# In a fused attention and MoE kernel, the second chunk's scores move behind the previous pair's values

## Chip, cores and metric

The kernel runs on one core of a Trainium2 chip. The metric is the device time of one execution in microseconds (us). PE is TensorE, ACT ScalarE, DVE VectorE, POOL GpSimd, SP SyncE.

## The reference

Three stages in float32: attention of 4 batches x 12 heads (448 tokens, 64 wide) with a tanh cap on the scores; a mixture of 8 experts, one for each of the 1792 tokens; and a soft mixture with 32 slots.

```python
def _attn_ref(q, k, v, cap):
    scale = 1.0 / np.sqrt(q.shape[-1])
    scores = scale * np.matmul(q, k.transpose(0, 1, 3, 2))
    scores = cap * np.tanh(scores / cap)
    scores = scores - np.max(scores, axis=-1, keepdims=True)
    attn = np.exp(scores)
    attn = attn / (np.sum(attn, axis=-1, keepdims=True) + 1e-09)
    return np.matmul(attn, v).astype(np.float32)
...
    attn_out = _attn_ref(**attn_kwargs)
    x = np.ascontiguousarray(attn_out.transpose(0, 2, 1, 3)).reshape(B * S, H * D)
    x = _moe_ref(x=x, **moe_kwargs)
    return _moe2_ref(x=x, **moe2_kwargs)
```

The MoE stage takes each token's expert by the largest logit of x @ w_gate plus a bias, and multiplies gate * relu(x @ w1) @ w2.

## The kernel before, in words

The order of the instructions on each engine is the order in which the program is written; every engine works its queue in that order and waits on semaphores.

Attention goes over 24 pairs of heads (`for p in range(NPAIR)` in `attention`, 6 pairs a batch). Scores are held transposed: 448 keys by 448 queries, the keys in chunks of 128. Chunks 0, 1 and 2 are full; what is left of both heads, 64 keys each, is one short chunk. `scores(p, c, dst)` makes one chunk: q and k are each split into a high and a low part (`split`, on DVE), and a score is the sum of three products (kh and qh, kh and ql, kl and qh), for a full chunk one matmul per head, so six. They go into a tile of `ps_s`, a PSUM pool with two buffers; then ACT applies tanh (line 571) from there into SBUF. After two chunks one exp goes over both (`pexp`, line 574): over chunks 0 and 1 into `pt`, over the short chunk and chunk 2 into `pm`.

One turn p of the loop gives PE, in this order:

1. `scores1(p)`: chunk 0, chunk 1, and on ACT the exp of both;
2. `pv(p - 1)` (line 606): the values of the pair before, six matmuls, the chunks 0, 1, 2 for two heads, into `o_ps`. Chunks 0 and 1 read `pt`, chunk 2 reads `pm`. `ps_o` has one buffer;
3. `post2(p - 2)`: row sums and gate logits (`r_ps`, line 488), a transpose of the values (`x_ps`, line 495);
4. `pv2(p - 1)` (line 610): the values of the short chunk;
5. `scores2(p)`: the short chunk; a transpose (`rt_ps`, line 501); `scores3(p)`: chunk 2 and the exp of `pm`.

DVE has in a turn: `adds2(p - 1)` (adds chunk 2's exp), `split(p + 1)`, the copy of `r_ps`, `adds1(p)` (adds the exps of chunks 0 and 1, so it waits for `pexp`), `post1(p - 1)` (line 614: empties `o_ps`), and `post3` (line 503 on), which scales x; SP stores x and then loads q, k and v of a pair two turns ahead. In PSUM `ps_s` takes four banks, `ps_m` two, `ps_o` and `ps_x` one each.

When a batch's six pairs are done, `route_batch` gives four steps of routing (logits, best expert, ranks, a selection matrix `bsel`) that are put into the following turns; three batches fall into the loop, the fourth behind it.

Behind attention stand the experts (`item`), which split their weights in the same way and multiply three times, and then the soft mixture, which streams weights of 768 KB a unit through a ring of buffers.

Of the kernel before, what the change touches and what calls it, by code (L numbers as in the profile page):

```python
# [9 lines left out]
F32 = mybir.dt.float32  # L10
# [42 lines left out]
def attn_moe_softmoe(ctx, tc, qT, kT, vP, cap, modality, w_gate, mod_bias, w1, w2, w2t, phi, m2_w1, m2_w2, out):  # L53
# [3 lines left out]
    B, NP_, _, HD, S = qT.shape  # L57
# [46 lines left out]
    def tt(out, in0, in1, op, eng=None):  # L104
        (eng or nc.vector).tensor_tensor(out=out, in0=in0, in1=in1, op=op)  # L105
# [110 lines left out]
    def m2_load(i, pieces=1):  # L216
        src, slot = m2_src(i), m2_slot(i)
        m2_tiles[i] = slot.rearrange("p (k f) -> p k f", f=512 if i < 4 * E else H2)
        if pieces == 1:
            nc.sync.dma_start(slot, src)  # L220
            return []
        h = UNIT // pieces
        return [call(nc.sync.dma_start, slot[:, h * k:h * k + h], src[:, h * k:h * k + h]) for k in range(pieces)]

    def call(f, *a):
        return lambda *b: f(*a, *b)
# [211 lines left out]
    a1 = Slices(arena)  # L438
# [8 lines left out]
    def gather(col, rows=None):  # L447

        lim = {} if rows is None else {"bounds_check": rows - 1, "oob_is_err": False}
        for i in range(NT):  # L450
            nc.gpsimd.indirect_dma_start(out=xg[:, i, :], out_offset=None, in_=x_dram if rows is None else x_dram[:rows],  # L451
                                         in_offset=bass.IndirectOffsetOnAxis(ap=idx[:, col + i:col + i + 1], axis=0),
                                         **lim)
# [89 lines left out]
    def weights_first():  # L543
        e_first.append(load_e(NI + 3))
        for s in range(NRW):
            wload("A", s, e_first[-1])

    def attention(a1, a1q, a2p, first, ps_s, ps_o, ps_x, ps_m, item_start):
        raw, spl, pt_t, pt_m, o_t, part = dict(first), {}, {}, {}, {}, {}

        def split(p):
            spl[p] = split_qk(a1q, *raw[p][:2])

        def product(ps, k, p, row_sets):
            qh, ql, kh, kl = spl[p]
            for t, (kk, qq) in enumerate(((kh, qh), (kh, ql), (kl, qh))):
                for o, r in row_sets(ps):
                    nc.tensor.matmul(o, lhsT=kk[r, k], rhs=qq[r], start=(t == 0), stop=(t == 2))  # L558

        def by_heads(ps):  # L560

            return [(ps[:, h, :S], slice(HD * h, HD * h + HD)) for h in range(2)]

        def together(ps):

            return [(ps[:, 0, :S], slice(0, 128))]

        def scores(p, c, dst):
            ps = ps_s.tile([128, 2, 512], F32, tag="s", name="s_ps")
            product(ps, slice(KC * c, KC * c + KC), p, by_heads if c < NKC else together)  # L570
            nc.scalar.activation(out=dst, in_=ps[:, :, :S] if c < NKC else ps[:, 0, :S], func=AF.Tanh)  # L571

        def pexp(t):
            nc.scalar.activation(out=t, in_=t, func=AF.Exp, scale=capb)  # L574

        def scores1(p):
            pt = pt_t[p] = a1.tile([128, 2, 2, S], F32, tag="pt", name="pt", bufs=3)
            for c in range(2):
                scores(p, c, pt[:, c])
            pexp(pt)  # L580

        def scores2(p):
            pt_m[p] = a1.tile([128, 3, S], F32, tag="pm", name="pm", bufs=3)
            scores(p, NKC, pt_m[p][:, 0])

        def scores3(p):
            scores(p, 2, pt_m[p][:, 1:3])
            pexp(pt_m[p])

        def adds1(p):  # L590

            part[p] = a1.tile([128, 2, S], F32, tag="t1", name="t1", bufs=3)
            tt(part[p], pt_t[p][:, 0], pt_t[p][:, 1], ALU.add)

        def adds2(p):
            t, m = part.pop(p), pt_m[p]
            tt(t, t, m[:, 1:3], ALU.add)
            sums[p] = [(onesel[:, 0], t[:, 0]), (onesel[:, 1], t[:, 1]), (onesel[:, 2], m[:, 0])]

        def pv(p):  # L600
            vt = raw[p][2]
            o = o_t[p] = ps_o.tile([128, S], F32, tag="o", name="o_ps")
            for c in range(NKC):
                for h in range(2):
                    hd = slice(HD * h, HD * h + HD)
                    nc.tensor.matmul(o[hd], lhsT=vt[:, c, hd], rhs=pt_t[p][:, c, h] if c < 2 else pt_m[p][:, 1 + h],  # L606
                                     start=(c == 0), stop=False)

        def pv2(p):
            nc.tensor.matmul(o_t[p], lhsT=raw[p][2][:, NKC], rhs=pt_m[p][:, 0], start=False, stop=True)  # L610

        def post1(p):
            xt = a1.tile([128, S], F32, tag="xt", name="xt", bufs=2)
            nc.vector.tensor_copy(xt, o_t.pop(p))
            xun[p] = xt

        extra = {0: late_consts, 1: call(set_guard, 1e-9 * math.exp(-CAP_SMALL)), 2: later_consts, 4: last_consts}
        extra.update({5 + i: call(nc.vector.memset, xg[:, i], 0.0) for i in range(NT)})
        extra[9] = zero_c
        n2 = 0  # L620
        spl[0] = first_split
        later = []
        for p in range(NPAIR):
            if p + 2 < NPAIR:
                raw[p + 2] = load_qkv(a1, a1q, p + 2)
            if p >= 4 and p % 2 == 0 and n2 < NRING + 1:
                m2_load(n2)
                n2 += 1
            scores1(p)
            if p >= 1:  # L630
                pv(p - 1)
                adds2(p - 1)
            if p + 1 < NPAIR:
                split(p + 1)
            if p >= 2:
                post2(p - 2, a1, ps_x, ps_m)
            if later:
                later.pop(0)()
            if p >= 1:
                pv2(p - 1)  # L640
            scores2(p)
            adds1(p)
            if p >= 1:
                post1(p - 1)
            if p >= 2:
                post3(p - 2, a1, ps_m)
            scores3(p)
            if p in extra:
                extra[p]()
            if later:  # L650
                later.pop(0)()
            if p >= 2 and (p - 2) % NP_ == NP_ - 1:
                b = (p - 2) // NP_
                rb = route_batch(b, a2p, ps_m)
                later += rb
                if b == NB1 - 1:
                    f = route_first(a2p, ps_m)
                    later[-2] = lambda: (rb[-2](), f[0]())
                    later += [f[1], lambda: [g() for g in f[3:-1] + f[2:3]], lambda: (f[-1](), gather(NA, NB1 * S), weights_first()),
                              lambda: None, lambda: None]  # L660
                later.pop(0)()
        while later:
            later.pop(0)()
        assert n2 == NRING + 1 and a1.end <= UNIT * (NRINGA - 1)
        wsplits, xpreps = item_start()
        wsplits[0]()
        xscale(NA, True)
        pv(LAST)
        adds2(LAST)
        post2(LAST - 1, a1, ps_x, ps_m)  # L670
        wsplits[1]()
        for f in xpreps[:3]:
            f()
        pv2(LAST)
        for f in xpreps[3:5]:
            f()
        post1(LAST)
        xpreps[5]()

    def load_qkv(a1, a1q, p, eng=None):  # L680
        b, hp = divmod(p, NP_)
        qr = a1q.tile([128, S], F32, tag="qr", name="qr", bufs=2)
        kr = a1q.tile([128, S + KL], F32, tag="kr", name="kr", bufs=2)
        vt = a1.tile([128, NKC + 1, 2 * HD], F32, tag="vt", name="vt", bufs=4)
        (eng or nc.sync).dma_start(kr, kT[b, hp])
        nc.sync.dma_start(qr, qT[b, hp].rearrange("h d s -> (h d) s"))
        nc.sync.dma_start(vt, vP[b, hp])
        return qr, kr, vt

    def split_qk(a1q, qr, kr, act=False):  # L690

        qh, ql, kh, kl = (a1q.tile([128, w], F32R, tag=n, name=n, bufs=2)
                          for n, w in (("qh", S), ("ql", S), ("kh", S + KL), ("kl", S + KL)))
        if act:
            nc.scalar.copy(kh, kr)
        else:
            nc.vector.tensor_copy(kh, kr)
        ts(qh, qr, qsc, ALU.mult)
        stt(ql, qr, qsc, qh.bitcast(F32), ALU.mult, ALU.subtract)
        tt(kl, kr, kh.bitcast(F32), ALU.subtract)  # L700
        return qh, ql, kh, kl
# [797 lines left out]
```

## Time and profile before

| | |
|---|---|
| runs shown, us | 528.33, 532.64, 536.36 (median 532.64) |
| the profiled execution, us | 529.52 |
| its span, first to last instruction, us | 527.8 |
| mean granted TensorE clock | 0.976 |
| busy in the span: PE, DVE, ACT, POOL | 90%, 52%, 47%, 14% |
| HBM traffic | 112.52 MB read, 11.71 MB written |

The span is what the trace covers; the execution's own time has 1.7 us more around it. Times in rows are us from the span's start. A busy share says how long an engine had work under way, not that it set the time. A group of rows writes `x12` for twelve instructions merged, the time in brackets is the engine's idle time before the row and what ended it. Float32 matmuls have two records each, so six matmuls of `pv` are x12. Ends of matmuls are modelled and overlap the next start; distances between starts are the measure.

### The profile page before, as it was taken

The numbers are of one execution on the slowest core, as the hardware profiler recorded it, in microseconds if no ns is written. First come the engines' busy times: TensorE is split into PE (matmuls) and PEld (weight loads), VectorE is DVE, ScalarE is ACT, GpSimd is POOL, SyncE is SP. The second block draws the span as 40 slices with busy tenths as digits, with TensorE's granted clock in tenths as the row PEclk, the third lists the DMA queues.
The fourth block names the chain that finished last, engine by engine and source line by source line (L and its number), as shares of the span: only waits on it lengthen the run. The fifth ranks groups of instructions, "written<-read, shape, count | busy, mean of one in ns | idle before, by whom it ended". The sixth has DMA issues, their size and how long they took to land. (4 is left out here: it accounts for less than half of the span.)

```text
span 527.8 us, 10800 instructions
## 1 busy us (share of the span) xinstructions
PE 477.2 (90%) x4179; PEld 301.9 (57%) x4179; DVE 275.8 (52%) x706; ACT 247.2 (47%) x353; POOL 71.7 (14%) x141
## 2 busy tenths in 40 slices
PE   7999999999999998999688999999999989996673
PEld 5455555555555564687565777677767755531231
DVE  4769899688878966477331435143513323001323
ACT  5887877877878767132322325233532331100222
POOL 2000000000000022226213223121012104110000
PEclk9999999999999999999889999999999999996988
DMA  6264655634425229768939995978387989999998
GB/s 201 88 146 151 209 171 151 210 95 130 141 88 148 81 80 286 221 217 263 280 87 290 332 296 195 288 225 298 114 292 256 334 326 409 415 413 414 416 408 308
DMA packets 57944, 124.99 MB, mean 237 GB/s; under 512 B 9385, under 2 KB 29040, under 8 KB 57888
## 3 DMA queue, kind: packets, MB, share of 16 engines
q1 hardware_dynamic: 55488, 117.54, 65.1%
q0 software_dynamic: 2256, 6.71, 4.5%
q8 instruction: 34, 0.56, 0.4%
q14 instruction: 22, 0.18, 0.1%
q10 hardware_dynamic: 144, 0.00, 0.0%
HBM read 112.52 MB, written 11.71 MB: 235 GB/s over the span
## 5 line engine op out<-in xcount | busy, mean ns | idle before, releaser
L571 ACT ACTIVATE arena<-s_ps 128x896 f32<-128x896 f32 (+1 forms) x96 | 75.9, 817 | 43.9 <-PE s_ps L558 43.9
L787 PE MATMUL acc_ps<-xh,wh 128*128 128x468 f32 x192 | 77.3, 403 | 1.4 <-DVEq L1175 1.2
L574 ACT ACTIVATE arena<-arena,capb 128x1792 f32<-128x1792 f32 (+1 forms) x48 | 77.0, 1604 | 1.6
L105 DVE TENSOR_TENSOR wl<-rw,wh 128x384 fp32r<-128x384 f32 x44 | 24.6, 560 | 101.5 <-ACT wh L740 85.0
L788 PE MATMUL acc_ps<-xl,wh 128*128 128x468 f32 x192 | 72.6, 378 | 0.0
L789 PE MATMUL acc_ps<-xh,wl 128*128 128x468 f32 x192 | 72.2, 376 | 0.0
L105 DVE TENSOR_TENSOR arena<-arena 128x896 f32<-128x896 f32 x48 | 52.3, 1089 | 28.5 <-ACT arena L574 27.1
L606 PE MATMUL o_ps<-arena 128*64 128x448 f32 x288 | 59.6, 548 | 1.1 <-ACT arena L574 0.6
L740 ACT CAST wh<-rw 128x384 fp32r<-128x384 f32 x64 | 32.4, 507 | 57.7 <-issue 20.5
L558 PE MATMUL s_ps<-qh,kh 64*128 64x448 f32 (+1 forms) x168 | 49.4, 483 | 10.2 <-ACT arena L571 9.4
L451 POOL DMA_INDIRECT xg<-x_dram,idx x16 | 18.2, 1138 | 223.9 <-PE s_ps L558 179.5
L913 ACT ACTIVATE h<-acc_ps 128x468 f32<-128x468 f32 x32 | 17.9, 560 | 56.9 <-PE acc_ps L789 56.8
L787 PEld LDWEIGHTS acc_ps<-xh,wh 128*128 128x128 f32 x192 | 36.6, 191 | 13.5 <-issue 7.0
L789 PEld LDWEIGHTS acc_ps<-xh,wl 128*128 128x128 f32 x192 | 36.5, 190 | 4.6
L788 PEld LDWEIGHTS acc_ps<-xl,wh 128*128 128x128 f32 x192 | 36.7, 191 | 3.4
L558 PEld LDWEIGHTS s_ps<-qh,kh 64*128 64x128 f32 (+1 forms) x168 | 18.4, 188 | 33.3 <-ACT arena L571 19.6
L606 PEld LDWEIGHTS o_ps<-arena 128*64 128x64 f32 x288 | 18.5, 136 | 30.9 <-issue 26.2
L558 PE MATMUL s_ps<-qh,kl 64*128 64x448 f32 (+1 forms) x168 | 35.8, 368 | 0.0
L558 PE MATMUL s_ps<-ql,kh 64*128 64x448 f32 (+1 forms) x168 | 35.6, 367 | 0.0
L105 POOL TENSOR_TENSOR wl<-rw,wh 128x384 fp32r<-128x384 f32 x20 | 21.2, 1060 | 77.9 <-ACT wh L740 77.8
L805 PE MATMUL h_ps<-ident,h 128*117 128x128 f32 x128 | 22.3, 296 | 1.0 <-ACT htok L808 1.0
L488 PEld LDWEIGHTS r_ps<-arena,onesel 128*32 128x32 f32 x576 | 13.3, 109 | 16.3 <-issue 13.4
(259 smaller groups left out, 695.0 us busy)
## 6 DMA issues: line engine op xcount, KB each, us to landing
ring<-in_moe_w_dram SPq DMA_DIRECT2D x30, 768.0 KB
w2r<-in_moe_w2t_dram SPq DMA_DIRECT2D x32, 384.0 KB
w2r<-in_moe_w_dram SPq DMA_DIRECT2D x28, 384.0 KB
arena<-in_moe_w_dram SPq DMA_DIRECT2D x13, 768.0 KB
rw<-in_moe_w_dram SPq DMA_DIRECT2D x24, 384.0 KB
arena<-in_moe_w_dram SPq DMA_DIRECT2D x22, 384.0 KB
arena<-in_v_dram SPq DMA_DIRECT2D x24, 256.0 KB
kr<-in_k_dram SPq DMA_DIRECT2D x23, 256.0 KB
```

Source lines behind the costliest of these rows:

```text
L105: (eng or nc.vector).tensor_tensor(out=out, in0=in0, in1=in1, op=op)
L451: nc.gpsimd.indirect_dma_start(out=xg[:, i, :], out_offset=None, in_=x_dram if rows is None else x_dram[:rows], in_offset=bass.IndirectOff ...
L558: nc.tensor.matmul(o, lhsT=kk[r, k], rhs=qq[r], start=(t == 0), stop=(t == 2))
L571: nc.scalar.activation(out=dst, in_=ps[:, :, :S] if c < NKC else ps[:, 0, :S], func=AF.Tanh)
L574: nc.scalar.activation(out=t, in_=t, func=AF.Exp, scale=capb)
L606: nc.tensor.matmul(o[hd], lhsT=vt[:, c, hd], rhs=pt_t[p][:, c, h] if c < 2 else pt_m[p][:, 1 + h], start=(c == 0), stop=False)
L740: nc.scalar.copy(wh, rw)
L787: nc.tensor.matmul(ps, lhsT=wh, rhs=hi[k], start=(k == 0), stop=False)
L788: nc.tensor.matmul(ps, lhsT=wh, rhs=lo[k], start=False, stop=False)
L789: nc.tensor.matmul(ps, lhsT=wl, rhs=hi[k], start=False, stop=(k == total - 1))
L805: nc.tensor.transpose(tp[:, i], h[:, W * i:W * i + W], ident)
L913: nc.scalar.activation(out=big["h"][n % NHB], in_=acc.pop(n), func=AF.Relu)
```

## The change

`scores1` now does one chunk a call, and the call for chunk 1 stands behind `pv(p - 1)`. The exp of both chunks still follows the tanh of chunk 1. `adds2(p - 1)` keeps its place behind both calls. In the first pair (p = 0) there are no values before, and nothing changes. No instruction is added or taken away.

```diff
-        def scores1(p):
-            pt = pt_t[p] = a1.tile([128, 2, 2, S], F32, tag="pt", name="pt", bufs=3)
-            for c in range(2):
-                scores(p, c, pt[:, c])
-            pexp(pt)
+        def scores1(p, c):
+            if c == 0:
+                pt_t[p] = a1.tile([128, 2, 2, S], F32, tag="pt", name="pt", bufs=3)
+            scores(p, c, pt_t[p][:, c])
+            if c:
+                pexp(pt_t[p])
...
-            scores1(p)
+            scores1(p, 0)
             if p >= 1:
                 pv(p - 1)
+            scores1(p, 1)
+            if p >= 1:
                 adds2(p - 1)
```

In the changed kernel lines behind this place have numbers higher by one (to 628) or three. On ACT, DVE, POOL and SP the instructions stand in the same order as before; on PE they move.

PE in an ordinary turn, before: `s_ps_772` is chunk 0, `s_ps_780` chunk 1, `o_ps` the values, `r_ps` the row sums, `x_ps` the transposes.

```order
L558 MATMUL s_ps_772<-qh_712,kh_714 128x448 x2
L558 MATMUL s_ps_772<-ql_713,kh_714 128x448 x2
L558 MATMUL s_ps_772<-qh_712,kl_715 128x448 x2
L558 MATMUL s_ps_780<-qh_712,kh_714 128x448 x2
L558 MATMUL s_ps_780<-ql_713,kh_714 128x448 x2
L558 MATMUL s_ps_780<-qh_712,kl_715 128x448 x2
L606 MATMUL o_ps_789<-arena_71 64x448 x6
L488 MATMUL r_ps_805<-arena_71,onesel_85 32x112 x12
L488 MATMUL r_ps_805<-arena_71,wg_86 32x112 x4
L495 MATMUL x_ps_822<-ident_83,arena_71 112x128 x4
```

The same turn in the changed kernel, where `s_ps_787` is chunk 1:

```order
L558 MATMUL s_ps_772<-qh_712,kh_714 128x448 x2
L558 MATMUL s_ps_772<-ql_713,kh_714 128x448 x2
L558 MATMUL s_ps_772<-qh_712,kl_715 128x448 x2
L607 MATMUL o_ps_780<-arena_71 64x448 x6
L558 MATMUL s_ps_787<-qh_712,kh_714 128x448 x2
L558 MATMUL s_ps_787<-ql_713,kh_714 128x448 x2
L558 MATMUL s_ps_787<-qh_712,kl_715 128x448 x2
L488 MATMUL r_ps_805<-arena_71,onesel_85 32x112 x12
L488 MATMUL r_ps_805<-arena_71,wg_86 32x112 x4
L495 MATMUL x_ps_822<-ident_83,arena_71 112x128 x4
```

The six matmuls of values have passed in front of chunk 1; the row sums and all behind them stand where they stood.

PE in turn 1, where no row sums exist yet, before: `s_ps_324` is chunk 0, `s_ps_332` chunk 1.

```order
L558 MATMUL s_ps_324<-qh_281,kl_284 128x448 x2
L558 MATMUL s_ps_332<-qh_281,kh_283 128x448 x2
L558 MATMUL s_ps_332<-ql_282,kh_283 128x448 x2
L558 MATMUL s_ps_332<-qh_281,kl_284 128x448 x2
L606 MATMUL o_ps_341<-arena_71 64x448 x6
```

And in the changed kernel (`s_ps_339` is chunk 1):

```order
L558 MATMUL s_ps_324<-qh_281,kl_284 128x448 x2
L607 MATMUL o_ps_332<-arena_71 64x448 x6
L558 MATMUL s_ps_339<-qh_281,kh_283 128x448 x2
L558 MATMUL s_ps_339<-ql_282,kh_283 128x448 x2
L558 MATMUL s_ps_339<-qh_281,kl_284 128x448 x2
```

Here too chunk 1 comes to PE six matmuls later.

## Rows read from the trace of the kernel before

**Rows 1.** Busy time by stage: window, its length, engines with instructions, PEclk, DMA share, GB/s.

```profile
0.00:200.00 200.00, 188.30 (x1685) 108.60 (x1686) 157.09 (x365) 150.34 (x147) 8.36 (x31) 1.00 0.48 141
200.00:397.00 197.00, 183.30 (x1425) 135.98 (x1421) 86.52 (x242) 70.33 (x145) 44.85 (x52) 0.98 0.77 246
397.00:527.80 130.80, 105.56 (x1076) 57.37 (x1073) 32.18 (x100) 26.57 (x61) 18.52 (x59) 0.93 0.94 370
```

**Rows 2.** Waits of 20 to 200 us: waiting, for whom, us in total, times, longest.

```profile
PE s_ps L558 <- ACT arena L571: 8.4, 21, 0.4
```

**Rows 3.** Timeline of PE in an ordinary pair: start, length, instruction, idle before.

```profile
107.24 0.47 PE L558 MATMUL s_ps<-qh,kh 64*128 64x448 f32 x2
...
108.36 0.36 PE L558 MATMUL s_ps<-qh,kl 64*128 64x448 f32 x2
109.13 0.47 PE L558 MATMUL s_ps<-qh,kh 64*128 64x448 f32 x2 [0.41 <-ACT arena L571]
109.44 0.37 PE L558 MATMUL s_ps<-ql,kh 64*128 64x448 f32 x2
109.64 0.36 PE L558 MATMUL s_ps<-qh,kl 64*128 64x448 f32 x2
109.93 2.48 PE L606 MATMUL o_ps<-arena 128*64 128x448 f32 x12
112.34 0.78 PE L488 MATMUL r_ps<-arena,onesel 128*32 128x112 f32 x24
...
114.88 0.37 PE L558 MATMUL s_ps<-qh,kl 128*128 128x448 f32 x1
...
115.29 0.47 PE L558 MATMUL s_ps<-qh,kh 64*128 64x448 f32 x2
```

**Rows 4.** Timeline of ACT in the same pair.

```profile
109.11 1.42 ACT L574 ACTIVATE arena<-arena,capb 128x1344 f32<-128x1344 f32 x1
110.43 1.71 ACT L571 ACTIVATE arena<-s_ps 128x896 f32<-128x896 f32 x2
112.17 1.79 ACT L574 ACTIVATE arena<-arena,capb 128x1792 f32<-128x1792 f32 x1
115.29 0.55 ACT L571 ACTIVATE arena<-s_ps 128x448 f32<-128x448 f32 x1 [1.32 <-PE s_ps L558]
```

**Rows 5.** Timeline of DVE in the same pair: both additions of exps, the copy of `o_ps`.

```profile
110.56 1.09 DVE L105 TENSOR_TENSOR arena<-arena 128x896 f32<-128x896 f32 x1 [2.01 <-ACT arena L574]
...
114.00 1.09 DVE L105 TENSOR_TENSOR arena<-arena 128x896 f32<-128x896 f32 x1
115.01 0.62 DVE L614 COPY arena<-o_ps 128x448 f32<-128x448 f32 x1
```

**Rows 6.** Timeline of PE at the last pair's values.

```profile
203.34 0.97 PE L606 MATMUL o_ps<-arena 128*64 128x448 f32 x4 [0.60 <-ACT arena L574]
```

**Rows 7.** Timeline of ACT there.

```profile
201.87 1.41 ACT L574 ACTIVATE arena<-arena,capb 128x1344 f32<-128x1344 f32 x1
```

**Rows 8.** Timeline of PE in a pair with a batch's routing.

```profile
84.22 0.37 PE L558 MATMUL s_ps<-qh,kl 64*128 64x448 f32 x2
...
85.79 0.60 PE L606 MATMUL o_ps<-arena 128*64 128x448 f32 x2
```

**Rows 9.** Timeline of DVE there: the copy of `o_ps`, the next addition of exps.

```profile
84.48 0.62 DVE L614 COPY arena<-o_ps 128x448 f32<-128x448 f32 x1
...
86.42 1.09 DVE L105 TENSOR_TENSOR arena<-arena 128x896 f32<-128x896 f32 x1 [0.36 <-ACT arena L574]
```

**Rows 10.** Timeline of ACT in pair 1.

```profile
14.81 1.71 ACT L571 ACTIVATE arena<-s_ps 128x896 f32<-128x896 f32 x2
16.55 1.79 ACT L574 ACTIVATE arena<-arena,capb 128x1792 f32<-128x1792 f32 x1
18.38 0.55 ACT L571 ACTIVATE arena<-s_ps 128x448 f32<-128x448 f32 x1
```

**Rows 11.** Timeline of PE in pair 1.

```profile
13.20 0.36 PE L558 MATMUL s_ps<-qh,kl 64*128 64x448 f32 x2
...
14.31 2.48 PE L606 MATMUL o_ps<-arena 128*64 128x448 f32 x12
```

## The prediction

> **What bounds the kernel now.** I read first the table by stage [rows 1]. The first 200 us are attention: PE is busy 188 of them at a granted clock of 1.00 (the upper of the two levels), with DMA at 0.48, so neither the clock nor the loads hold this stage. The change touches this stage alone. Then the waits of 20 to 200 us [rows 2]: the one recurring stop of PE's matmuls is a score matmul behind a tanh of ACT, 21 times 0.4 us. To see what it costs, I read one ordinary pair on three engines [rows 3 to 5]. It starts, for me, at 107.24, when PE begins chunk 2 of the pair before, and the next one starts at 115.29: a period of 8.05 us.
>
> In that period PE does chunk 2, then chunk 0 of the next pair (its last product starts at 108.36), and then stands. Chunk 1 wants the PSUM buffer that chunk 2 filled, and ACT reads that buffer until 109.1, when the exp starts behind it [rows 4]. Products that follow each other without a wait are 0.20 apart (109.44 to 109.64), so chunk 1 could have begun at 108.56; it begins at 109.13, and its second product comes 0.31 behind the first and not 0.20. The stop costs 0.57 + 0.11 = 0.68 us a pair. Then come the values of pair p - 1 at 109.93 and the row sums at 112.34.
>
> **The change part by part.** No instruction is added or removed; on PE six matmuls of values pass in front of the six of chunk 1. Four things follow.
>
> *The old wait goes.* By the time the values are done (three chunks in 112.34 - 109.93 = 2.41 us, 0.80 each), the buffer of chunk 2 has been free for long. Gain: 0.68 us a pair.
>
> *A new wait comes.* The values of pair p - 1 use chunk 2's exp as their third operand. Now they start 0.29 after chunk 0's last product (the distance from 109.64 to 109.93), at 108.36 + 0.29 = 108.65, and reach their third chunk two chunks later, at 110.25. The exp of chunk 2 starts at 109.11 and takes 1.42 [rows 4], so it ends at 110.53, and a matmul that waits for ACT starts 0.06 behind it: in the tail the same exp ends at 201.87 + 1.41 = 203.28 and the third chunk's values start at 203.34 [rows 6, 7]. That is 110.59, a wait of 0.34; with half of a restart of 0.11 I take 0.40. Behind this matmul PE's queue holds chunk 1, the row sums and the rest of the pair, and ACT waits for chunk 1.
>
> *One more change of shape.* Between products of equal shape PE steps by 0.20; where scores (64*128) give way to values (128*64) it is 0.29 [rows 3]. Before, chunk 1 stood next to chunk 0, of its own shape; now it stands between values and row sums, which is one more such change in a pair. I take 0.10, between 0.09 and the restart of 0.11; below, nothing at all, if it hides under a slow matmul of values.
>
> The Trainium skill speaks against the change at this place: TensorEngine Tiling (Array Packing), section Key Properties, says that a switch of the tiling mode, unlike a switch of the tile, drains TensorE. The step of 0.29 against 0.20 agrees with it; the page gives no price; with a drain for each switch a pair saves the 0.18 below, and without one it would be 0.28.
>
> So an ordinary pair saves 0.68 - 0.40 - 0.10 = 0.18 us. Of the 21 stops [rows 2] three fall into pairs that are not ordinary (below): 18 x 0.18 = 3.2 us gained. The bounds of one pair are 0.34 (no change of shape, no restart) and 0.08.
>
> *Chunk 1's tanh, its exp and all behind them come later.* Before, the tanh of chunk 1 starts right behind that of chunk 0, at about 111.25 in [rows 4], since its scores have long been there. Now the values' third chunk starts at about 110.65 and ends at 111.45; chunk 1's last product starts some 0.5 later (a shape change and two steps) and a tanh starts 0.41 behind a last product (114.88 to 115.29 in [rows 3, 4]): 112.3, so 1.05 later. Where is the cover?
> - ACT has 1.32 us of idle before the next short chunk's tanh [rows 4], so it still gets there in time in an ordinary pair.
> - DVE adds up the exps at 114.00 and then empties the values' only PSUM buffer by 115.01 + 0.62 = 115.63 [rows 5], 8.39 after the period's start. Plus 1.05 that is 9.44, or 1.57 in the next period of 7.87. The values would start 108.65 - 107.24 = 1.41 into it: late by 0.2 with the wake-up. In an ordinary pair this is hidden, because the third chunk would wait 0.34 in any case.
> - The idle 2.01 of DVE before 110.56 shrinks to about 0.9. The loads of K, Q and V of pair p + 2, which SP issues behind the store of x, come about 1 us later; they are asked for a whole pair ahead, and I count them as nothing. If that cover were gone, a pair would wait for as much as they are late.
>
> *Where that cover is missing.* Three times in the loop (for the batches 0, 1 and 2) DVE also does a batch's routing, and its work has no gap over two pairs. In the first of these the copy starts at 84.48 and ends at 85.10, and only at 86.42 has DVE caught up [rows 9]; the values started at 85.79, 0.69 behind the copy [rows 8]. Now they could start at 84.22 + 0.29 = 84.51, but the copy would be some 0.9 later too (1.05 less one shorter period): 85.10 + 0.9 - 84.51 = 1.5 us of wait. The old stop of 0.68 goes there as well and the third chunk then finds its exp ready, so with the shape change the pair loses 1.5 + 0.1 - 0.68, about 0.9: three times, 2.7 us. Bounds of one: 0.5, if DVE regains some of its lateness, and 1.6, if nothing of the old stop is saved.
>
> *The start.* In pair 1 ACT is what bounds: its instructions stand back to back from 14.81 to 18.38 and beyond [rows 10]. There the values (14.31) now start at 13.20 + 0.29 = 13.49 [rows 11], end at about 15.9, chunk 1's last product starts near 16.3 and its tanh at 16.7, and before it was 0.80 behind 14.81, at 15.6. ACT loses 1.0 us that nothing makes good; bounds 0.5 and 1.1.
>
> **The sum**: -3.2 + 1.0 + 2.7 = +0.5 us at the end of attention. Bounds: -18 x 0.34 + 0.5 + 1.5 = -4.1 and -18 x 0.08 + 1.1 + 4.8 = +4.5. The code behind attention is the same, and I let the shift pass through it. On the profiled execution of 529.52 us (span 527.8 and 1.7 around it) that makes 530.0. The runs shown are 528.33, 532.64 and 536.36, so the profiled one lies 3.1 below their median; I forecast 531.5, halfway between 530.0 and 532.64 + 0.5 = 533.1.
>
> **The rivals.**
> *A, the new waits are small (a gain).* If the routing pairs and the start lose little and an ordinary pair saves 0.34, then 21 x 0.34 = 7.1 less 0.5: 6.6 us, 525 us on the forecast's base. For it speaks that PE is the busy engine and DVE idle for 2.01 in each pair; against it, that DVE has no idle time at all in the routing pairs. Only if the exp of chunk 2 were also ready in time would all 0.68 go: 14 us, 517; the rows put it 0.34 too late.
> *B, the values' single PSUM buffer decides every pair (slower).* The copy on DVE now hangs on chunk 1's exp of the same pair, and its end, 1.57 into the period, is 0.2 late already. The third chunk hides lateness up to about 0.35. From there each tenth more costs 21 x 0.1 = 2.1 us; a copy later by 0.5 than I worked out (a slower tanh or exp behind a drained PE) loses the 0.18 and another 0.35 in each pair: 21 x 0.35 + 3.7 = 11 us, 542. Half of that lateness, 0.25, gives about 537.
> *C, nothing arrives.* The last 131 us have DMA at 0.94 [rows 1]; if the weights' stream sets the end whatever attention does, the time stays at that of before, 531 on the same base.
>
> **How the numbers follow.** Forecast 0.58, A 0.15 (0.03 of it with the whole 0.68), B 0.17 (0.05 of it beyond 2%), C 0.10. A difference of 2%, 10.6 us, is about what a measurement of this kernel can tell from no change: 0.03 faster, 0.92 within it, 0.05 slower. The range runs from 526 (nearly A's 525) to 538 (past B's half case): the bounds of the sum around 531.5 give 526.9 to 535.5, and the executions of before alone scatter by 8.
>
> **What would show it right or wrong.** In the changed profile PE's 21 waits of chunk 1 are gone, and in their place the values stand behind ACT's exp, some 0.35 each, or in three pairs 1 to 1.6 behind DVE's copy. The period of ordinary pairs is 7.8 to 7.95, and the end of attention moves by under 2 us. DVE's idle before its second addition falls from 2.01 to about 0.9. Periods at or over 8.05 everywhere, with PE waiting for DVE, mean B; periods of 7.7 with no wait in the routing pairs mean A; and a shift at the end of attention that the total doesn't show means C.

## The result, and the profile after

The changed kernel takes 534.06 us (median of 12 runs, 531.79 to 538.58); before, beside it, 531.71 (12 runs, 528.33 to 536.36). The ratio is 1.0062 (95%: 1.0037 to 1.0087): slower by 0.6%, some 3.3 us (2.0 to 4.6; the two medians lie 2.35 apart). The profiled execution took 535.37, its span is 533.6. By stage, with the columns of [rows 1]:

```profile
0.00:200.00 200.00, 189.08 (x1659) 104.86 (x1663) 155.40 (x363) 150.40 (x146) 6.03 (x28) 1.00 0.45 136
200.00:397.00 197.00, 181.76 (x1430) 135.21 (x1422) 86.94 (x241) 71.89 (x145) 46.80 (x54) 0.98 0.76 242
397.00:533.60 136.60, 111.77 (x1107) 60.93 (x1098) 33.19 (x102) 27.50 (x63) 19.10 (x60) 0.90 0.95 368
```

Clock and DMA share of attention are what they were (1.00; 0.45 after 0.48). The waits of 20 to 200 us, with the columns of [rows 2]:

```profile
PEld o_ps L607 <- ACT arena L574: 14.8, 20, 1.0
PEld o_ps L607 <- DVE arena L615: 12.5, 18, 1.9
...
PE o_ps L607 <- DVE arena L615: 3.9, 4, 1.6
...
PE s_ps L558 <- ACT arena L571: 0.9, 1, 0.9
...
PE o_ps L607 <- ACT arena L574: 0.6, 3, 0.2
PE rt_ps L501 <- DVE arena L108: 0.2, 1, 0.2
```

The 21 stops of [rows 2] are down to one. In their place the values wait, mostly with the weight load ahead of a matmul (PEld): 20 times with the exp as the last to come, 18 times with the copy of `o_ps`. PEld overlaps PE, so these totals are no loss in themselves; what they cost is read from distances between starts. One ordinary pair on PE, for [rows 3]:

```profile
109.52 0.47 PE L558 MATMUL s_ps<-qh,kh 64*128 64x448 f32 x2
109.82 0.36 PE L558 MATMUL s_ps<-ql,kh 64*128 64x448 f32 x2
...
110.22 0.37 PE L558 MATMUL s_ps<-qh,kh 64*128 64x448 f32 x2
...
110.63 0.37 PE L558 MATMUL s_ps<-qh,kl 64*128 64x448 f32 x2
111.13 2.69 PE L607 MATMUL o_ps<-arena 128*64 128x448 f32 x12
113.76 0.47 PE L558 MATMUL s_ps<-qh,kh 64*128 64x448 f32 x2
114.06 0.36 PE L558 MATMUL s_ps<-ql,kh 64*128 64x448 f32 x2
114.27 0.36 PE L558 MATMUL s_ps<-qh,kl 64*128 64x448 f32 x2
114.56 0.78 PE L488 MATMUL r_ps<-arena,onesel 128*32 128x112 f32 x24
...
117.51 0.47 PE L558 MATMUL s_ps<-qh,kh 64*128 64x448 f32 x2
```

The period is 117.51 - 109.52 = 7.99 us, 8.00 from exp to exp, 0.05 under the 8.05 of before; 7.87 was forecast. The values start 0.50 and not 0.29 behind chunk 0, because the copy of `o_ps` is late; inside the row of twelve, the third chunk starts at 112.85 (single records), behind the exp. Then chunk 1: 113.76, 114.06, 114.27, row sums at 114.56. ACT and DVE in this pair, for [rows 4] and [rows 5]:

```profile
111.38 1.42 ACT L574 ACTIVATE arena<-arena,capb 128x1344 f32<-128x1344 f32 x1
112.70 0.90 ACT L571 ACTIVATE arena<-s_ps 128x896 f32<-128x896 f32 x1
114.67 0.92 ACT L571 ACTIVATE arena<-s_ps 128x896 f32<-128x896 f32 x1 [1.06 <-PE s_ps L558]
115.62 1.79 ACT L574 ACTIVATE arena<-arena,capb 128x1792 f32<-128x1792 f32 x1
117.51 0.55 ACT L571 ACTIVATE arena<-s_ps 128x448 f32<-128x448 f32 x1
```

```profile
109.45 1.09 DVE L105 TENSOR_TENSOR arena<-arena 128x896 f32<-128x896 f32 x1 [1.25 <-ACT arena L574]
110.46 0.62 DVE L615 COPY arena<-o_ps 128x448 f32<-128x448 f32 x1
...
112.83 1.09 DVE L105 TENSOR_TENSOR arena<-arena 128x896 f32<-128x896 f32 x1 [0.79 <-ACT arena L574]
```

ACT's idle time has moved from before the short chunk's tanh (1.32, [rows 4]) to between its two long tanhs (1.06); DVE's of 2.01 in [rows 5] is 0.79, with 1.25 now ahead of the other addition. The copy runs from 110.46 to 111.08, and the values follow it 0.05 later.

A turn with routing, for [rows 8] and [rows 9], first PE (the end of chunk 0, the values), then DVE:

```profile
85.63 0.36 PE L558 MATMUL s_ps<-qh,kl 64*128 64x448 f32 x2
87.36 2.48 PE L607 MATMUL o_ps<-arena 128*64 128x448 f32 x12 [1.38 <-DVE arena L615]
```

```profile
85.72 1.06 DVE L105 TENSOR_TENSOR arena<-arena 128x896 f32<-128x896 f32 x1
86.69 0.62 DVE L615 COPY arena<-o_ps 128x448 f32<-128x448 f32 x1
```

The values could start at 85.63 + 0.29 and start at 87.36, 1.44 later, behind a copy that itself stands behind an addition on a DVE without a gap. And pair 1 on ACT, for [rows 10]:

```profile
15.02 0.90 ACT L571 ACTIVATE arena<-s_ps 128x896 f32<-128x896 f32 x1
17.03 0.92 ACT L571 ACTIVATE arena<-s_ps 128x896 f32<-128x896 f32 x1 [1.11 <-PE s_ps L558]
17.98 1.79 ACT L574 ACTIVATE arena<-arena,capb 128x1792 f32<-128x1792 f32 x1
```

Two tanhs that stood back to back are now 1.11 apart, on the engine that bounds this pair. Of that 0.69 reaches the exp of chunk 2 in this pair.

How attention's shift is made up I read from the starts of the 24 exps of chunk 2 on ACT (one a pair). The last of them goes from 201.87 [rows 7] to 205.45, +3.57:

| part of the loop | period before, after (us) | shift |
|---|---|---|
| pair 0 (nothing changed there) | | +0.21 |
| pairs 1 and 2 (in pair 2 the values wait 0.37 for the copy) | 6.65 to 7.34; 8.07 to 8.49 | +1.11 |
| turns 8, 10, 16, 22, 23 (DVE has routing, or is behind from it) | 8.46 to 8.85; 8.05 to 9.01; 8.05 to 8.28; 10.75 to 11.93; 8.72 to 9.07 | +3.11 |
| the 16 other turns | 8.05 to 8.00 (turns 14 and 20, with routing: 8.46 to 8.40) | -0.86 |

PE's own waits for the copy of `o_ps` stand in turns 2, 10, 16 and 22 (0.37, 1.38, 0.63 and 1.56). In turn 8 PE waits 0.23 for a transpose's operand, the copy of `r_ps`, which DVE reaches late.

The first expert matmul then starts 3.57 later (210.66 to 214.24), and the span ends 5.85 later; the timed 3.3 agrees with attention's part. The other 2.3 us of this one execution lie behind attention, where the last stage's granted clock is 0.90 and was 0.93.

### The profile page after: what moved, and what is told of

Same layout as the page of the kernel before. It is cut to its first block, busy times and chain, and to the rows that moved or that the text cites. A ratio compares the mean times of both kernels' runs of the same rounds, so it can differ in the third digit from the quotient of the medians.

```text
span 533.6 us, 10800 instructions
## 1 busy us (share of the span) xinstructions
PE 482.6 (90%) x4179; PEld 301.0 (56%) x4179; DVE 275.5 (52%) x706; ACT 249.8 (47%) x353; POOL 71.9 (13%) x141
## 5 line engine op out<-in xcount | busy, mean ns | idle before, releaser
L571 ACT ACTIVATE arena<-s_ps 128x896 f32<-128x896 f32 (+1 forms) x96 | 78.5, 820 | 44.8 <-PE s_ps L558 41.6
L607 PE MATMUL o_ps<-arena 128*64 128x448 f32 x288 | 63.4, 554 | 8.2 <-DVE arena L615 3.9
L607 PEld LDWEIGHTS o_ps<-arena 128*64 128x64 f32 x288 | 16.9, 135 | 44.7 <-ACT arena L574 17.1
L611 PE MATMUL o_ps<-arena 128*128 128x448 f32 x48 | 22.5, 550 | 0.0
```

## The experiments

In the expectations T is the account above: an ordinary pair gains almost nothing because of the exp's wait and the change of shape, and the start and the routing turns lose. B and C are the prediction's rivals. The results, all against the kernel before, timed beside each. Shifts are of the profiled executions, in us, counted from the exp of pair 0, which no kernel changes and which lies between -0.54 and +0.21:

| kernel | ordinary period, us | last exp of attention | first expert matmul | time, ratio (95%) |
|---|---|---|---|---|
| changed | 8.00 | +3.36 | +3.36 | 1.0062 (1.0037 to 1.0087) |
| e1_copy_first | 8.00 | +0.13 | +0.33 | 1.0032 (1.0002 to 1.0061) |
| e2_third_behind | 7.72 | -0.05 | -0.05 | 0.9957 (0.9924 to 0.9990) |
| e3_both | 7.72 | -3.70 | -3.38 | 0.9863 (0.9824 to 0.9903) |
| e4_sums_between | 7.57 | -7.87 | -4.06 | 0.9937 (0.9903 to 0.9970) |
| e5_sums_copy | 7.57 | -9.52 | -8.47 | 0.9772 (0.9729 to 0.9815) |
| e6_old_in_some | 8.00 | +0.01 | +0.01 | 1.0004 (0.9967 to 1.0041) |
| e8_delay | 8.05 | +6.63 | +12.52 | 1.0171 (1.0132 to 1.0209) |
| e10_w2_later | 7.57 | -9.49 | -9.17 | 0.9820 (0.9778 to 0.9861) |

**Is it the values' single buffer (rival B)?** e1_copy_first is the changed kernel with the copy of `o_ps` ahead of the addition of exps on DVE, so that the copy no longer hangs on the exp of chunk 1:

```diff
-            adds1(p)
             if p >= 1:
                 post1(p - 1)
+            adds1(p)
```

> The changed kernel, with DVE's copy of the values' PSUM buffer ahead of the addition of chunk 0's and 1's exps. Theory T (the values' third chunk waits for chunk 2's exp, and the scores of chunk 1 cost two changes of shape; the copy costs only in the turns with routing): ordinary period stays at 8.00 us, since the third chunk's wait grows by what the copy's wait loses; the losses of 0.4 to 1.2 us in the turns with routing shrink to under half, the end of attention comes 1.5 to 2.5 us earlier than in the changed kernel, total about 1.002 of before. Rival B (the single buffer of values, emptied late, sets every pair): ordinary period falls by 0.2 to 7.8, attention ends 4 us or more earlier than in the changed kernel, total under before by 0.3% or more.

Time 533.15. PE in an ordinary pair (end of chunk 0, values, chunk 1, row sums):

```profile
108.19 0.37 PE L558 MATMUL s_ps<-qh,kl 64*128 64x448 f32 x2
108.49 1.72 PE L607 MATMUL o_ps<-arena 128*64 128x448 f32 x8
110.42 0.97 PE L607 MATMUL o_ps<-arena 128*64 128x448 f32 x4 [0.20 <-ACT arena L574]
111.32 0.47 PE L558 MATMUL s_ps<-qh,kh 64*128 64x448 f32 x2
111.63 0.36 PE L558 MATMUL s_ps<-ql,kh 64*128 64x448 f32 x2
111.82 0.37 PE L558 MATMUL s_ps<-qh,kl 64*128 64x448 f32 x2
112.12 0.78 PE L488 MATMUL r_ps<-arena,onesel 128*32 128x112 f32 x24
```

Now the values start on time (0.30 behind chunk 0) and the third chunk stands for the exp instead: same period, 8.00. So in ordinary pairs the late copy decides nothing, as forecast. The turns with routing are another matter: turns 8, 10, 16 and 22 go from 8.85, 9.01, 8.28 and 11.93 to 8.41, 8.00, 8.00 and 10.78, pair 2 from 8.49 to 8.05, and attention ends 3.23 us earlier than in the changed kernel (1.5 to 2.5 was expected). There the copy's place on DVE is the cause. B holds in a few turns only.

**What the exp's wait and a change of shape cost.** e2_third_behind puts only the first two chunks of the values ahead of chunk 1's scores, the third behind them (`pv` gets a list of chunks):

```diff
-                pv(p - 1)
+                pv(p - 1, (0, 1))
             scores1(p, 1)
             if p >= 1:
+                pv(p - 1, (2,))
                 adds2(p - 1)
```

> The changed kernel, with the third chunk of the values moved behind chunk 1's scores, so that it finds chunk 2's exp ready. Theory T: the wait of 0.17 and its restart go, chunk 1's tanh comes about 0.9 us earlier and with it the copy, so the values' start (0.21 late) is free too; one more change of shape comes in. From chunk 0's last product to the row sums 0.29 + 1.65 + 0.31 + 0.20 + 0.29 + 0.43 + 0.48 = 3.65 us, where the changed kernel has 3.93 and before 3.98: period 7.7, total 5 to 7 us under before. Rival S (changes of shape cost more than the wait, 0.3 each): period 8.0 or more, total at or over before. Rival L (the loss lies behind attention): total over before although attention ends earlier.

Time 529.89. The same stretch of PE:

```profile
108.37 0.37 PE L558 MATMUL s_ps<-qh,kl 64*128 64x448 f32 x2
108.66 1.72 PE L609 MATMUL o_ps<-arena 128*64 128x448 f32 x8
110.32 0.47 PE L558 MATMUL s_ps<-qh,kh 64*128 64x448 f32 x2
110.62 0.36 PE L558 MATMUL s_ps<-ql,kh 64*128 64x448 f32 x2
110.82 0.37 PE L558 MATMUL s_ps<-qh,kl 64*128 64x448 f32 x2
111.12 0.97 PE L609 MATMUL o_ps<-arena 128*64 128x448 f32 x4
112.02 0.78 PE L488 MATMUL r_ps<-arena,onesel 128*32 128x112 f32 x24
```

No row has a wait, and the period is 7.72: 0.28 less than in the changed kernel, though there is one change of shape more. Of the changed kernel's waits 0.38 are gone (0.21 for the copy, 0.17 for the exp), and 0.10 goes to that change. The start loses more than in the changed kernel (+2.13 by pair 2), and turns 10, 16 and 22 take 9.29, 8.73 and 11.45, so attention ends where it did before the change (-0.05). The time is 2.3 us under before, where 5 to 7 were expected. e3_both has both edits:

> The changed kernel with both edits: the third chunk of values behind chunk 1's scores, and the copy of the values' buffer ahead of the addition on DVE. Theory T: ordinary period 7.72 as with the third chunk alone (the copy is in time there), and the waits for the copy in the turns with routing (1.5 us and less) shrink to under half: attention ends 2 to 4 us before that of before. Rival B (only the copy matters): no more than the copy alone gave, 8.00 a period.

Time 526.34. The two add up: at the end of attention e1 is 3.23 ahead of the changed kernel, e2 3.41, both together 7.06.

**A filler that waits for nothing.** e4_sums_between has the values where they were before and puts the row sums of pair p - 2 between the two chunks of scores (`row_sums` is the part of `post2` that fills `r_ps`; `post2` takes its tile from `r_early`):

```diff
             scores1(p, 0)
-            if p >= 1:
-                pv(p - 1)
+            if p >= 2:
+                r_early[p - 2] = row_sums(p - 2, ps_m)
             scores1(p, 1)
             if p >= 1:
+                pv(p - 1)
                 adds2(p - 1)
```

> The order of before, with the row sums of pair p - 2 (0.9 us of PE, which need nothing recent) between chunk 0 and chunk 1. Theory T: they fill the 0.57 us stop for chunk 2's buffer, chunk 1 is still done before ACT wants it (its tanh keeps its place right behind chunk 0's), no operand of the values is late and the copy keeps its margin of over 2 us; a change of shape more costs 0.2. Period 7.65, total 6 to 8 us under before (0.985 to 0.989). Rival S (changes of shape cost as much as the stop): 8.0 to 8.1 and no difference. Rival L (time won in attention is lost behind it): attention ends 7 us earlier, the total moves by under 2.

Time 527.67. PE from chunk 0's last product through the sums to chunk 1:

```profile
111.67 0.37 PE L563 MATMUL s_ps<-qh,kl 64*128 64x448 f32 x2
111.97 0.78 PE L487 MATMUL r_ps<-arena,onesel 128*32 128x112 f32 x24
112.57 0.38 PE L487 MATMUL r_ps<-arena,wg 128*32 128x112 f32 x8
112.88 0.47 PE L563 MATMUL s_ps<-qh,kh 64*128 64x448 f32 x2
```

The period is 7.57: of the old stop of 0.68, 0.48 is saved, and 0.20 goes to the change of shape. Attention ends 7.87 earlier, but the first expert matmul only 4.06, and the ratio of 0.9937 misses the 0.985 to 0.989 expected. Behind attention ACT, which scales the gathered rows of the first experts, waits for their DMA, which it does not in the kernel before:

```profile
199.82 0.93 ACT L459 ACTIVATE xg<-xg,gsl 117x768 f32<-117x768 f32 x1 [1.74 <-DMA xg<-x_dram,idx]
```

**Where the loss sits.** e6_old_in_some is the changed kernel with the old order in pairs 0 to 2 and in the turns at and behind each batch's routing (8 to 10, 14 to 16, 20 to 23):

```diff
+            old = p in (0, 1, 2, 8, 9, 10, 14, 15, 16, 20, 21, 22, 23)
             scores1(p, 0)
+            if old:
+                scores1(p, 1)
             if p >= 1:
                 pv(p - 1)
-            scores1(p, 1)
+            if not old:
+                scores1(p, 1)
```

> The changed order in 11 ordinary turns only (3 to 7, 11 to 13, 17 to 19); the order of before at the start, in the turns around a batch's routing and in the last ones. Theory T: the losses at the start (1.3 us) and at the routing (3.1 us) go and 11 x 0.05 us of gain are left: attention ends within 1 us of before, total 0.998 to 1.002 of before. Rival L (the loss of 0.6% does not come from these turns): the total stays 2 us or more over before.

Time 532.13. The loss of the start is gone, those of turns 16 and 22 too, and turn 10 takes 8.17; the other turns have their 8.00. Turn 8 still takes 8.85: in the old order itself, it follows five turns in the new one that leave DVE later, and PE waits there for the copy of `r_ps` (0.18). From pair 0 to the end of attention the sum is nil (+0.01). So the new order in these 11 turns gains 0.05 a turn, 0.56 in all, and turns 8 and 10 alone give 0.51 back; turns 14, 16 and 20 give back nothing.

**Does attention's end reach the total (rival C)?** e8_delay is the kernel before with 32 matmuls into an unread tile, between chunk 1 and the values of turn 11:

```diff
             scores1(p)
+            if p == 11:
+                idle = ps_m.tile([128, 96], F32, tag="sm", name="idle_ps")
+                for _ in range(32):
+                    nc.tensor.matmul(idle, lhsT=ident, rhs=onesel.rearrange("p a b -> p (a b)"), start=True, stop=True)
```

> The kernel before, with 32 more matmuls (float32, 96 columns, into a PSUM tile that nobody reads) on PE in turn 11, between the scores of chunk 1 and the values: about 3.5 us of PE and nothing else. It asks whether a later end of attention reaches the end of the kernel. Theory T (the shift of attention is the loss that was timed): attention ends 3 to 4 us later, total 1.005 to 1.008 of before, as with the changed kernel. Rival C (what happens behind attention hides the shift): attention ends 3 to 4 us later, the total moves by less than 1.5 us (under 1.003).

Time 543.24. The delay is twice what I meant, since each of these matmuls has two records too:

```profile
93.95 7.38 PE L633 MATMUL idle_ps<-onesel,ident 128*128 128x96 f32 x64
```

Attention ends 6.63 later and the time is 1.71% or 9.1 us longer, even more than was put in. C falls, for a delay of this size: the stream of weights hides no delay of attention. The extra is behind attention; one place is the gather, for which ACT waits here as well:

```profile
216.66 0.94 ACT L459 ACTIVATE xg<-xg,gsl 117x768 f32<-117x768 f32 x1 [3.62 <-DMA xg<-x_dram,idx]
```

**The version that beats both kernels.** e5_sums_copy is e4 with the copy ahead of the addition as in e1:

> Row sums between chunk 0 and chunk 1, and the copy ahead of the addition on DVE. Theory T: ordinary period 7.57 as without the second edit; in the turns with routing the row sums no longer wait for the copy (1.7 us in all), so attention ends 9 to 10.5 us before that of before; of the additional 1 to 2 us little reaches the end, since the gather of the first experts' rows, not attention, then holds PE. Total 0.989 to 0.994. Rival (DVE itself is what bounds the turns with routing): attention ends at the same time as without the second edit.

Time 522.99, ratio 0.9772: the fastest kernel of the study, 2.3% under the kernel before. Attention ends 1.64 earlier than in e4, the first expert matmul 4.41; the wait for the gather is 0.93, where it was 1.74. That little of this would reach the end (0.989 to 0.994) was wrong. e10_w2_later takes e5 and issues the first w2 loads, which are under way beside the gather, behind the second call that loads w1 (`w2rest` is the loop that is taken out):

```diff
-            for j in range(NR2):
-                w2load(j, e_first[-1])
-            return [call(wfirst, s) for s in range(AHEAD)], [call(xprep, k, "aat"[k % 3]) for k in range(KD)]
+            return [call(wfirst, 0), lambda: (wfirst(1), w2rest())], [call(xprep, k, "aat"[k % 3]) for k in range(KD)]
```

> As the run with row sums between and the copy first, and SP issues the four first loads of w2 behind the fifth load of w1, so that they don't share the DMA engines with the gather of the first experts' rows. Theory G (behind the shorter attention the gather lands late because 1.5 MB of w2 loads run beside it): PE's 2.4 us wait for the scaled rows shrinks to under 1, the first expert matmul comes 6.5 to 8.5 us earlier than in before (it was 4.6 with row sums between), total 1 to 2 us less than that run. Rival (the gather itself takes that long, or the late w2 loads hold the first product with phi): the first expert matmul moves by under 1 us, or PE then waits for w2.

Time 523.94, not separable from e5 (0.9778 to 0.9861 against 0.9729 to 0.9815). The gather's wait falls to 0.21 and the first expert matmul gains 0.70, but PE then waits for w2, as its products with it show:

```profile
204.96 0.63 PE L773 MATMUL wphi_ps<-w2r,phi_sb 128*32 128x256 f32 x6 [1.27 <-DMA w2r<-in_moe_w2t_dram]
...
206.41 0.63 PE L773 MATMUL wphi_ps<-w2r,phi_sb 128*32 128x256 f32 x6 [0.82 <-DMA w2r<-in_moe_w2t_dram]
```

So, in one execution of each, the gather lands earlier without these loads beside it, and moving them only moves the wait.

## Why the prediction was wrong

**The sign.** The working gave +0.5 us at the end of attention, with bounds of -4.1 and +4.5, which hold the measured +3.3 (and the trace's +3.57). The forecast of 531.5 nevertheless lay below the median shown, 532.64, because I put it halfway towards the profiled execution. That read as "no change, if anything faster"; added to the median the same sum would have read as slightly slower. A sum is a difference, and belongs on the same base as what it is compared with.

**The step that failed: "One more change of shape ... I take 0.10".** It is 0.20. In e1's rows the third chunk starts at 110.42; its two passes take 0.38 each and the first 0.05 more behind a wait, so chunk 1 could start 0.80 later. It starts 0.90 later (0.10 for the change), and its second product comes 0.31 behind the first and not 0.20 (another 0.11; the trace has that product's weight load begin 0.10 behind the first product and not together with it). What follows chunk 1 now costs what followed the values before, 0.09 and 0.10. I had both numbers, took them for two guesses at one cost, and chose between them; they add up. The 0.31 I had put down to the old stop alone, but the first step of each group of scores shows it without any wait (109.52 to 109.82 above). e4 gives the same 0.20 in another way: 0.68 saved less 0.48 that arrives. The rule of the Trainium skill that I cited (TensorEngine Tiling (Array Packing), Key Properties: a switch of the tiling mode drains) agrees with the late first product, 0.90 for 0.80.

**The exp's wait, forecast 0.40.** It is 0.43: 0.38 of wait, counted from when the values could have started, and the 0.05 of the pass behind it. The third chunk starts 3.34 after the period's start, and 3.35 was forecast; but the first two chunks pass in 1.55 and not 1.60 (my 0.80 a chunk was an average that held the change of shape behind the third). So an ordinary pair saves 0.68 - 0.43 - 0.20 = 0.05 and not 0.18: over 18 pairs 2.3 us less than forecast, most of what the sum missed.

**The start, forecast +1.0.** +1.11, and that it came so near is in part luck. ACT's gap of 1.11 stands in pair 1 where I looked for it, but only 0.69 of it reaches the exp of chunk 2: ACT was not back to back to the end, it had stood 0.27 before the tanh of chunk 2 (at 19.19 before the change). The other 0.42 is pair 2, which I had not counted; there the values wait 0.37 for the copy, and e1, with the copy first, has 8.05.

**The routing turns, forecast +2.7 over three pairs.** +3.11 over five turns. The three that I meant (10, 16 and 22) lose 0.96, 0.23 and 1.18, 2.37 in all; PE waits there 1.38, 0.63 and 1.56 for the copy (1.44 against the earliest start in turn 10, where 1.5 was worked out). Turns 8 and 23, which I had left out, lose another 0.74. The mechanism was right and e1 shows it by taking it away: there these turns are at or near the periods of before, turn 23 excepted (9.13), whose loss stays unexplained. Corrected, the terms are -0.86 + 1.11 + 3.11 = +3.36, and with the 0.21 by which pair 0 of the two executions differs, the 3.57 of the trace.

**Cover.** The copy late by 0.2 in ordinary pairs is 0.21 and costs nothing there, as e1 shows; DVE's idle time of "about 0.9" is 0.79. Of the signs given, the period of 7.8 to 7.95 (8.00) and an end of attention that moves by under 2 us (3.57) failed, and one of the three waits for the copy (0.63) lies under the 1 to 1.6.

**The rivals.** A: no. B: not in ordinary pairs. C: no, by e8.

**What stays open** is the size of what happens behind attention. In e4 7.87 us gained in attention give 3.4 in the time (0.63%); e5 has 1.64 more and gives 12 (2.28%); 6.63 us of delay in e8 give 9.1; e1 and e2 end attention nearly as before does (+0.13, -0.05), and one is 0.3% slower, the other 0.4% faster. Part may lie in the base: e3, e5, e8 and e10 ran on another chip than e1, e2, e4 and e6, and the kernel before took 533.95 on the first (11 runs) and 531.51 on the second (35). The times of e4 and e5 as they stand are 4.7 apart, near the 4.41 between their first expert matmuls; no run tells the chips apart. Part is the gather's landing (waits of 0 to 3.62). The nearer the first w2 load is issued behind the last gather, the longer ACT waits: 2.6 us behind it in the kernel before, no wait; 2.1 in e3, 0.21; 2.0 in e5, 0.93; 0.8 in e4 and e8, 1.74 and 3.62. That is a pattern of single executions and no shown cause, and the rest I have not followed through the stage that streams weights.

## What to carry to other kernels

Fill a wait on TensorE with work whose operands are long ready (here the row sums of two pairs back), not with work whose last operand is being made by the very engine that causes the wait. Before you move work on one engine, follow each single buffer that it frees or fills through the other engine's queue: here a copy behind an addition cost 3.2 us in a few turns, most of them where that engine has no gap, and swapping two calls took that back. And count a change of matmul shape with both of its parts, the late first product and the slow second one.

## What was unexpected of the hardware

- A change of shape into scores (64*128) costs 0.20 net: first product 0.10 late, second 0.11, less 0.01 at the row sums behind. It is as much as one of the 0.20 products.
- A shift at the end of attention reached the total by 0.4 to 1.4 times its size (e4: 7.87 gives 3.4; e8: 6.63 gives 9.1; two chips), with waits of the gather from 0 to 3.62 us beside loads that are issued in the same program order.
- A full-width float32 matmul of 96 columns takes 0.23 us (7.38 us for 32, in 64 records that start 0.113 apart): each of a float32 matmul's two records takes time of its own.
